# Attention with a decay bias and two MLP layers: no bias tile, the mask written into the broadcast sum, query tiles from last to first

## The chip, the cores and the metric

One core of a Trainium2 chip runs the whole program. The metric is the device time of one execution in microseconds; the median of several runs counts. TensorE (PE) does the matrix products and transposes, VectorE (DVE), ScalarE (ACT) and GpSimd (POOL) the elementwise work, and SyncE (SP) issues all DMAs.

## The reference, cut to what matters

```python
# q, k, v: (4, 8, 576, 64), s: (4, 8, 576), float32
scores = 1/sqrt(64) * q @ k^T
cum  = cumsum(maximum(s, 0))                  # along the sequence
bias = -(cum[..., :, None] - cum[..., None, :])
scores = where(causal, -1e9, scores + minimum(bias, 0.0))
attn = exp(scores - max(scores)); attn /= sum(attn) + 1e-9
x = (attn @ v)  ->  (2304, 512)
y = (sigmoid(x @ w_gate) * (x @ w_val)) @ w_out        # d_ff 1536
h = y @ w_in                                            # d_ff 2048
out = (h - tanh(h)) @ w_out2
```

`cum` never falls along the sequence, so for every key that the causal mask leaves, the bias is at most zero and the minimum changes nothing. And a term that is the same for all keys of one query drops out of the softmax.

## The kernel before

The weights are 64-bit words; a `Conversion` turns each into a pair of fp32r parts (high and low), one unit of 128x512 per tick: two passes on ScalarE (L96, L82), three on VectorE (L88, L89, L91) and one on GpSimd (L83). The first conversion has 24 units (`w_gate`, `w_val`); its ticks are spread over the first 32 attention steps (`CONV_AT`).

Attention runs in 64 units (batch, query group, head). Group 0 holds queries 0 to 255 as two tiles, t = 0 and 1, against 256 keys; group 1 holds queries 256 to 575 as three tiles, t = 2, 3, 4, against 576 keys. All units of group 0 come first, batch by batch, then those of group 1. A tile is a step; there are 160. A tile t sees `width(t)` = 128, 256, 384, 512 or 576 keys, and only its last 128 columns need the causal mask. The loop over steps is written out by hand, and each engine gets its instructions in that order. In iteration i the program issues:

- VectorE: `eps(i-1)`, the score pass `ttr(i)` (L236: product in PSUM plus bias tile, scaled by -0.125, with the running minimum), `recip(i-1)`, `norm(i-1)`, the evacuation `evac(i-2)` of the transposed probabilities into a low part (L287, after ScalarE's high part L286), `nb(i+2)`, then `gt` of a gate product (L363), `xp` of a finished unit (L316), and the conversion's passes.
- GpSimd: `norm(i-1)` for t = 3 and 4 (L259; VectorE does it for the others, L261), the causal select of `nb(i+2)` (L206), the splits of x, v, k and q (L325, L186, L168, L172), and the conversion's low part (L83).
- ScalarE: high part of `evac(i-2)`, `exp(i)` (L243), `xtmp` (L315), high parts of the splits, the conversion's passes.
- TensorE: `qk(i+1)` (L223, L224), one or two gate or value products (`moe`, L347 to L351) of the batch finished last, the transposes `tr(i-1)` (L273), and the value product `pv` (L300) of a unit whose last evacuation has been issued. After the first 16 steps the transposes of all steps share one bank (bank 6), so `tr(i-1)` waits for `evac(i-2)` as well as for `norm(i-1)`.

The bias tile is made by `nb(i)` in two instructions: VectorE computes min(c - cum_i, 0) from `c`, the broadcast cumulative sum (loaded once per unit, three buffers), and `cumn`, a column of negated sums; GpSimd then fills the masked triangle of the last 128 columns. The sums are scaled by 8 (L379) to undo the factor of 0.125 on the way. `cumn` is made once, by five transposes of `cum` on TensorE (L384) and a copy on VectorE (L390). The transposed probabilities of a unit lie in one pair of buffers (`NPT = 1`) of five slots; group 0 uses slots 0 and 3, and relies on zeros in the part of slot 3 that no query of the first tile sees.

After attention come the rest of the products of the last batch, the output projection with conversion of `w_out` and `w_in` (to about 600 us), and the second layer.

Of the kernel before, what the change touches and what calls it, by code (L numbers as in the profile page):

```python
# [21 lines left out]
GRP = ((0, 256, (0, 1)), (256, 320, (2, 3, 4)))  # L22
MASK = -8.0e9
LN = 1
NSP = 3
# [13 lines left out]
def NORM(G, t):  # L39
    return "pool" if t > 2 else "dve"  # L40
# [3 lines left out]
def attention_moe_moe2(ctx: ExitStack, tc: tile.TileContext, kqT, v, s, wg, wv, wo, win, wo2, out):  # L44
# [11 lines left out]
    class Conversion:  # L56
        """float64 words to an exact pair of float32r parts of the float32 value, one unit per tick in three stages"""
# [138 lines left out]
    def nb(i):  # L196
        if i >= len(steps):
            return
        u, t = steps[i]
        b, G, h = units[u]  # L200
        w = width(t)
        n = at.tile([128, S], F, tag="nb", name="nb", bufs=3)[:, :w]
        c = U_[u]["c"][:, 0:w]
        j = b * H + h
        DVE.tensor_scalar(out=n, in0=c, scalar1=cumn[:, t, j:j + 1], scalar2=0.0, op0=ALU.add, op1=ALU.min)  # L205
        POOL.affine_select(out=n[:, w - 128:w], in_=n[:, w - 128:w], pattern=[[-1, 128]], base=0,  # L206
                           channel_multiplier=1, compare_op=ALU.is_ge, fill=MASK)
        T_[i] = {"nb": n}

    def qk(i):  # L210
# [8 lines left out]
        T_[i]["qk"] = []  # L219
# [7 lines left out]
    def ttr(i):  # L227
# [6 lines left out]
        for k, (ps, c0, c1) in enumerate(e.pop("qk")):  # L234
            init, acc = acc, e["nm"][:, k:k + 1]
            DVE.tensor_tensor_reduce(out=sp[:, c0:c1], in0=ps[:, 0:c1 - c0], in1=e["nb"][:, c0:c1],  # L236
# [39 lines left out]
    def evac(i):  # L276
# [8 lines left out]
        js = slice(0, t + 1) if G else slice(0, 3 * t + 1, 3)  # L285
# [5 lines left out]
    def pv(u):  # L291
# [5 lines left out]
        jobs = [(0, 0, 0), (1, 3, 0)] if G == 0 else [(0, 0, 0), (1, 1, 0), (2, 2, 0), (3, 3, 64), (4, 4, 64)]  # L297
# [77 lines left out]
    cumn = pt.tile([128, 5, 32], F, name="cumn")  # L375
    DVE.memset(zt, 0.0)
    DVE.tensor_scalar(out=sraw, in0=sraw, scalar1=0.0, scalar2=None, op0=ALU.max)
    DVE.tensor_tensor_scan(out=cum, data0=sraw, data1=zt, initial=0.0, op0=ALU.add, op1=ALU.add)
    DVE.tensor_scalar(out=cum, in0=cum, scalar1=8.0, scalar2=None, op0=ALU.mult)  # L379
    SP.dma_start(out=cscr, in_=cum)  # L380
    load_vc(0)
    ps = bank(6, [128, 5, 32])
    for t in range(5):
        PE.transpose(ps[:, t, :], cum[:, Q0[t]:Q0[t] + 128], ident[0:32, 0:32])  # L384
# [5 lines left out]
    DVE.tensor_scalar(out=cumn, in0=ps, scalar1=-1.0, scalar2=None, op0=ALU.mult)  # L390
    for _ in range(PRE):
        cvt.tick()
    nb(0)
    nb(1)
    split_v(0)
    split_kq(1)
    while parts:
# [7 lines left out]
    for i in range(n + LN + 1):  # L405
# [15 lines left out]
        if i < n:  # L421
            exp(i)
            nb(i + 2)
# [248 lines left out]
```

## Time and profile before

| | us |
|---|---|
| median of 3 runs (1157.55 to 1158.14) | 1157.69 |
| span of the profiled execution | 1156.5 |
| TensorE busy in it | 1063.0 |
| VectorE busy | 724.9 |
| ScalarE busy | 539.2 |
| GpSimd busy | 391.1 |

The profiled execution is one execution apart from the timed ones; its span runs from the first to the last instruction, and a run's time holds a little around that. Shares of busy time over the whole span say little here, because the stages have different limits; the views below are therefore cut by stretches: 0 to 136 us holds the first 32 steps with the conversion, 136 to 236 us the rest of group 0, 236 to 545 us group 1.

### The profile page before, as it was taken

How to read it: one execution, taken by the hardware profiler on the slowest of the kernel's cores; microseconds unless marked ns; L12 is line 12 of the kernel's file. 1: busy time of each engine (PE TensorE's matmuls, PEld its weight loads, DVE VectorE, ACT ScalarE, POOL GpSimd, SP SyncE). 2: the span in 40 equal slices, each digit the busy share in tenths (PEclk: the TensorE clock that was granted, in tenths of full speed). 3: DMA queues.
4: the chain of work that ended last, by engine and by line, in shares of the span. 5: the costliest groups of instructions: out<-in, count | busy, mean ns of one | idle time of the engine just before them, and what ended most of it. 6: DMA issues, size and time to landing. Idle time of an engine off the chain costs nothing.

```text
span 1156.5 us, 18998 instructions
## 1 busy us (share of the span) xinstructions
PE 1063.0 (92%) x6501; PEld 997.0 (86%) x6501; DVE 724.9 (63%) x1783; ACT 539.2 (47%) x1325; POOL 391.1 (34%) x524
## 2 busy tenths in 40 slices
PE   3457799989999999999899999999999999999998
PEld 2346699989899899898889999997899999999997
DVE  7999967688878788873856677378423233232322
ACT  4565556566666666653434444344323232232322
POOL 6786645466656566651311222023000000000000
PEclk9999999999999999999999999999999999999999
DMA  6556444443433433321746655233000000000000
GB/s 190 163 161 176 115 119 127 135 144 114 132 120 124 120 125 120 119 77 40 231 146 180 185 167 172 71 96 106 28 1 28 1 22 6 1 28 1 28 1 28
DMA packets 64417, 114.11 MB, mean 99 GB/s; under 512 B 7168, under 2 KB 40960, under 8 KB 64320
## 3 DMA queue, kind: packets, MB, share of 16 engines
q1 hardware_dynamic: 64320, 112.90, 31.8%
q8 instruction: 51, 0.84, 0.3%
q14 instruction: 46, 0.38, 0.1%
HBM read 93.92 MB, written 18.95 MB: 98 GB/s over the span
## 4 chain that ended last, share of the span: by engine, by line
PE 72%; DVE 15%; issue 5%; DMA 3%; ACT 3%; SPq 0%; POOL 0%; DVEq 0%; ACTq 0%; POOLq 0%
PE bank L605 15%; PE bank L348 6%; PE bank L347 6%; PE bank L351 6%; PE bank L581 5%; PE bank L582 5%; PE bank L585 5%; PE bank L300 4%; DVE raw L89 4%; PE bank L548 4%; PE bank L549 4%; PE bank L552 4%; PE bank L273 4%; PE bank L223 2%; DMA raw<-in_wo 2%
## 5 line engine op out<-in xcount | busy, mean ns | idle before, releaser
L588 DVE TENSOR_TENSOR th<-bank,th 128x384 f32<-128x384 f32 x96 | 53.5, 557 | 196.2 <-ACT th L587 196.1
L273 PE MATMUL bank<-ident,sp 128*128 128x128 f32 (+1 forms) x480 | 78.6, 273 | 68.8 <-DVE ptl L287 35.2
L286 ACT ACTIVATE pth<-bank 128x320 fp32r<-128x320 f32 (+2 forms) x160 | 69.6, 435 | 146.8 <-PE bank L300 88.1
L587 ACT ACTIVATE th<-bank 128x384 f32<-128x384 f32 x96 | 46.9, 488 | 192.0 <-PE bank L585 192.0
L273 PEld LDWEIGHTS bank<-ident,sp 128*128 128x128 f32 (+1 forms) x480 | 51.8, 143 | 86.6 <-DVE ptl L287 37.7
L243 ACT ACTIVATE sp<-sp,nm 128x576 f32<-128x576 f32 (+2 forms) x160 | 95.9, 599 | 45.0 <-DVE nm L236 44.8
L287 DVE TENSOR_TENSOR ptl<-bank,pth 128x320 fp32r<-128x320 f32 (+2 forms) x160 | 77.6, 485 | 49.0 <-ACT pth L286 33.0
L206 POOL TENSOR_SCALAR_AFFINE_SELECT nb<-nb 128x128 f32<-128x128 f32 x160 | 48.0, 300 | 150.9 <-DVE nb L205 115.1
L592 DVE TENSOR_TENSOR g2l<-th,g2h 128x384 fp32r<-128x384 f32 x96 | 53.6, 558 | 56.7 <-ACT g2h L591 56.7
L591 ACT ACTIVATE g2h<-th 128x384 fp32r<-128x384 f32 x96 | 50.4, 525 | 62.4 <-DVE th L588 62.4
L205 DVE TENSOR_SCALAR nb<-cbc,cumn 128x576 f32<-128x576 f32 (+2 forms) x160 | 76.6, 479 | 2.2 <-DMA cbc<-cum 2.2
L236 DVE CUSTOM_DVE_ANT_0 sp<-bank,nb 128x288 f32<-128x288 f32 (+2 forms) x160 | 75.6, 472 | 1.2 <-POOL nb L206 0.2
L223 PE MATMUL bank<-kh,qs 128*128 128x384 f32 (+1 forms) x192 | 70.7, 373 | 6.0 <-POOL qs L172 6.0
L89 DVE SCALAR_TENSOR_TENSOR raw<-raw 128x512 uint32<-128x512 uint32 x68 | 74.2, 1091 | 2.3
L496 DVE TENSOR_TENSOR gl<-g,gh 128x384 fp32r<-128x384 f32 x72 | 39.6, 556 | 57.3 <-PE bank L552 38.1
L261 DVE TENSOR_SCALAR sp<-sp,r 128x128 f32<-128x128 f32 (+1 forms) x96 | 72.6, 756 | 3.4
L168 POOL TENSOR_TENSOR kl<-kq,kh 128x256 fp32r<-128x256 f32 (+1 forms) x64 | 73.0, 1141 | 3.6 <-ACT kh L167 2.8
L300 PE MATMUL bank<-pth,vs 128*128 128x256 f32 (+1 forms) x224 | 71.2, 335 | 0.6 <-ACT pth L286 0.6
L495 ACT ACTIVATE gh<-g 128x384 fp32r<-128x384 f32 x72 | 37.1, 526 | 71.2 <-PE bank L549 60.8
L96 ACT ACTIVATE tmp<-raw 128x512 f32<-128x512 f32 x68 | 45.5, 669 | 46.6 <-DMA raw<-in_wo 26.8
L300 PE MATMUL bank<-ptl,vs 128*128 128x256 f32 (+1 forms) x224 | 64.7, 309 | 0.1
L91 DVE SCALAR_TENSOR_TENSOR tmp<-tmp,raw 128x512 uint32<-128x512 uint32 x68 | 59.9, 881 | 6.0 <-DVE raw L89 0.5
(588 smaller groups left out, 3405.3 us busy)
## 6 DMA issues: line engine op xcount, KB each, us to landing
kq<-in_kq SPq DMA_DIRECT2D x32, 448.0 KB, 3.6
raw<-in_wo SPq DMA_DIRECT2D x28, 512.0 KB, 3.6
g<-g SPq DMA_DIRECT2D x72, 192.0 KB, 3.4
cbc<-cum SPq DMA_DIRECT2D x32, 288.0 KB, 4.0
kq<-in_kq SPq DMA_DIRECT2D x32, 256.0 KB, 3.5
raw<-in_win SPq DMA_DIRECT2D x16, 512.0 KB, 3.6
g<-gt SPq DMA_DIRECT2D x48, 160.0 KB, 1.8
raw<-in_wg SPq DMA_DIRECT2D x12, 512.0 KB, 4.4
```

What stands on the lines that cost most here:

```text
L89: DVE.scalar_tensor_tensor(out=lo, in0=lo, scalar=29, in1=hi, op0=ALU.logical_shift_right, op1=ALU.bitwise_or)
L168: POOL.tensor_tensor(out=kl, in0=d["k"], in1=kh.bitcast(F), op=ALU.subtract)
L205: DVE.tensor_scalar(out=n, in0=c, scalar1=cumn[:, t, j:j + 1], scalar2=0.0, op0=ALU.add, op1=ALU.min)
L223: PE.matmul(ps, d["qs"][:, o:o + 128], d["kh"][:, c0:c1], start=True, stop=False)
L236: DVE.tensor_tensor_reduce(out=sp[:, c0:c1], in0=ps[:, 0:c1 - c0], in1=e["nb"][:, c0:c1], scale=-0.125, scalar=init, op0=ALU.add, op1=ALU. ...
L243: ACT.activation(out=e["sp"], in_=e["sp"], func=AF.Exp, scale=-1.0, bias=e["m"], accum_out=e["sum"])
L261: DVE.tensor_scalar(out=e["sp"], in0=e["sp"], scalar1=e["r"], scalar2=None, op0=ALU.mult)
L273: PE.transpose(ps[:, j, :], e["sp"][p0:128, c:c + 128], ident[p0:128, p0:128])
L286: ACT.activation(out=ph[:, js, o:o + n], in_=e["tr"], func=AF.Copy)
L287: DVE.tensor_tensor(out=pl[:, js, o:o + n], in0=e["tr"], in1=ph[:, js, o:o + n].bitcast(F), op=ALU.subtract)
L300: PE.matmul(ps[:, o:qw], d["vs"][:, j].rearrange("p a d -> p (a d)"), p[:, slot, o:qw], start=(n == 0 and m == 0), stop=(n == len(jobs) - ...
L605: PE.matmul(acc[t], g[:, t * 128:t * 128 + 128], w, start=(m == 0 and k == 0), stop=(m == M2 - 1 and k == 2))
```

## The change

- `nb` is gone, with `cumn`, its transposes, and the bias buffers. The score pass reads `c` itself: the sum of the query drops out of the softmax, and the minimum with zero does nothing where the mask leaves a key.
- The mask is written into `c` in place, one select per step as before (`mask(i+1)` in iteration i, ahead of `exp(i)`). So that a masked triangle hides no key that a later tile of the head needs, the tiles of a head go from last to first: 1, 0 and 4, 3, 2.
- All norms are on VectorE (`NORM`), those of t = 3 and 4 too.
- Group 0 uses slots 0 and 3 in even units and 1 and 4 in odd ones; a memset on GpSimd clears slot 4's part once at the start of group 1.
- The scaling by 8 moves into the maximum ahead of the cumulative sum, and MASK becomes a power of two. `sp` has five buffers instead of three.

```diff
-GRP = ((0, 256, (0, 1)), (256, 320, (2, 3, 4)))
-MASK = -8.0e9
+GRP = ((0, 256, (1, 0)), (256, 320, (4, 3, 2)))
+MASK = -(2.0 ** 33)
-NSP = 3
+NSP = 5
...
 def NORM(G, t):
-    return "pool" if t > 2 else "dve"
+    return "dve"
...
-    def nb(i):
-        if i >= len(steps):
-            return
-        u, t = steps[i]
-        b, G, h = units[u]
-        w = width(t)
-        n = at.tile([128, S], F, tag="nb", name="nb", bufs=3)[:, :w]
-        c = U_[u]["c"][:, 0:w]
-        j = b * H + h
-        DVE.tensor_scalar(out=n, in0=c, scalar1=cumn[:, t, j:j + 1], scalar2=0.0, op0=ALU.add, op1=ALU.min)
-        POOL.affine_select(out=n[:, w - 128:w], in_=n[:, w - 128:w], pattern=[[-1, 128]], base=0,
-                           channel_multiplier=1, compare_op=ALU.is_ge, fill=MASK)
-        T_[i] = {"nb": n}
+    def mask(i):
+        if i < len(steps):
+            u, t = steps[i]
+            w = width(t)
+            c = U_[u]["c"][:, w - 128:w]
+            POOL.affine_select(out=c, in_=c, pattern=[[-1, 128]], base=0, channel_multiplier=1,
+                               compare_op=ALU.is_ge, fill=MASK)
...
-            DVE.tensor_tensor_reduce(out=sp[:, c0:c1], in0=ps[:, 0:c1 - c0], in1=e["nb"][:, c0:c1],
+            DVE.tensor_tensor_reduce(out=sp[:, c0:c1], in0=ps[:, 0:c1 - c0], in1=U_[u]["c"][:, c0:c1],
...
-        js = slice(0, t + 1) if G else slice(0, 3 * t + 1, 3)
+        js = slice(0, t + 1) if G else slice(u % 2, u % 2 + 3 * t + 1, 3)
...
-    cumn = pt.tile([128, 5, 32], F, name="cumn")
     DVE.memset(zt, 0.0)
-    DVE.tensor_scalar(out=sraw, in0=sraw, scalar1=0.0, scalar2=None, op0=ALU.max)
+    DVE.tensor_scalar(out=sraw, in0=sraw, scalar1=0.0, scalar2=8.0, op0=ALU.max, op1=ALU.mult)
     DVE.tensor_tensor_scan(out=cum, data0=sraw, data1=zt, initial=0.0, op0=ALU.add, op1=ALU.add)
-    DVE.tensor_scalar(out=cum, in0=cum, scalar1=8.0, scalar2=None, op0=ALU.mult)
...
-    ps = bank(6, [128, 5, 32])
-    for t in range(5):
-        PE.transpose(ps[:, t, :], cum[:, Q0[t]:Q0[t] + 128], ident[0:32, 0:32])
...
-    DVE.tensor_scalar(out=cumn, in0=ps, scalar1=-1.0, scalar2=None, op0=ALU.mult)
...
-    nb(0)
-    nb(1)
+    mask(0)
...
+        if i - LN - 1 >= 0 and i - LN - 1 < n and steps[i - LN - 1] == (B * H, 4):
+            for p in pts[0]:
+                POOL.memset(p[:, 4, 128:256].bitcast(F), 0.0)
...
         if i < n:
+            mask(i + 1)
             exp(i)
-            nb(i + 2)
```

In the rows of the order below, the names after `<-` are what an instruction reads; `ISA` is the score pass and, in the row after it, the read of its minimum. First VectorE in the first batch, from the score pass of a unit's second tile to that of the next unit's first; before:

```order
L236 ISA sp,nm<-bank_399,nb 128x256
L236 ISA nm 128x1
L252 RECIPROCAL r<-sum 128x1
L261 TENSOR_SCALAR sp<-sp,r 128x128
L287 TENSOR_TENSOR ptl_156<-bank_402,pth_155 128x2x128
L205 TENSOR_SCALAR nb<-cbc,cumn 128x256
L88 TENSOR_SCALAR raw<-raw 128x512
L89 SCALAR_TENSOR_TENSOR raw<-raw 128x512
L91 SCALAR_TENSOR_TENSOR tmp<-tmp,raw 128x512
L247 TENSOR_SCALAR sum<-sum 128x1
L236 ISA sp,nm<-bank_421,nb 128x128
```

and after the change:

```order
L230 ISA sp,nm<-bank_374,cbc 128x128
L230 ISA nm 128x1
L246 RECIPROCAL r<-sum 128x1
L255 TENSOR_SCALAR sp<-sp,r 128x256
L281 TENSOR_TENSOR ptl_156<-bank_377,pth_155 128x128
L88 TENSOR_SCALAR raw<-raw 128x512
L89 SCALAR_TENSOR_TENSOR raw<-raw 128x512
L91 SCALAR_TENSOR_TENSOR tmp<-tmp,raw 128x512
L241 TENSOR_SCALAR sum<-sum 128x1
L230 ISA sp,nm<-bank_393,cbc 128x256
```

The nb row between the evacuation and the conversion is gone, the score pass reads `cbc` (the tile `c`), and the narrow tile comes second in the unit instead of the wide one.

Next GpSimd, one unit of the first batch, with the engines that each instruction waits for in brackets (`Activation` is ScalarE, `DMAHW` a load); before:

```order
L206 AFFINE_SELECT nb_684<-nb_684 128x128 [waits DVE_49]
L186 TENSOR_TENSOR vs_619<-vraw_546,vs_619 128x2x64 [waits DMAHW6_49,PE_49,Activation_49]
L168 TENSOR_TENSOR kl_696<-kq_620,kh_695 128x256 [waits DMAHW0_49,Activation_49]
L172 TENSOR_TENSOR qs_697<-kq_620,qs_697 64x256 [waits Activation_49,Pool_49]
L206 AFFINE_SELECT nb_726<-nb_726 128x128 [waits DVE_49,Pool_49]
L83 TENSOR_TENSOR w03l_95<-tmp_593,w03h_94 128x512 [waits Activation_49]
```

and after:

```order
L201 AFFINE_SELECT cbc_514<-cbc_514 128x128 [waits DVE_49]
L186 TENSOR_TENSOR vs_582<-vraw_513,vs_582 128x2x64 [waits DMAHW6_49,PE_49,Activation_49]
L168 TENSOR_TENSOR kl_655<-kq_583,kh_654 128x256 [waits DMAHW0_49,Activation_49]
L172 TENSOR_TENSOR qs_656<-kq_583,qs_656 64x256 [waits Activation_49,Pool_49]
L201 AFFINE_SELECT cbc_586<-cbc_586 128x128 [waits DMAHW1_49,Pool_49]
L83 TENSOR_TENSOR w03l_95<-tmp_558,w03h_94 128x512 [waits Activation_49]
```

The selects stand at the same places, but the first now waits for the score pass that reads the same `c`, and the second, which belongs to the next unit, waits for the load of its `c` and no longer for VectorE.

Last VectorE in group 1, two steps; before:

```order
L287 TENSOR_TENSOR ptl_156<-bank_6133,pth_155 128x4x128
L205 TENSOR_SCALAR nb<-cbc,cumn 128x576
L247 TENSOR_SCALAR sum<-sum 128x1
L236 ISA sp,nm<-bank_6171,nb 128x512
L236 ISA nm 128x1
L252 RECIPROCAL r<-sum 128x1
L261 TENSOR_SCALAR sp<-sp,r 128x384
L287 TENSOR_TENSOR ptl_156<-bank_6187,pth_155 128x5x64
L205 TENSOR_SCALAR nb<-cbc,cumn 128x384
L363 SCALAR_TENSOR_TENSOR gt<-th,bank_6174 128x320
```

and after:

```order
L230 ISA sp,nm<-bank_6085,cbc 128x512
L230 ISA nm 128x1
L246 RECIPROCAL r<-sum 128x1
L255 TENSOR_SCALAR sp<-sp,r 128x576
L281 TENSOR_TENSOR ptl_156<-bank_6088,pth_155 128x3x128
L241 TENSOR_SCALAR sum<-sum 128x1
L230 ISA sp,nm<-bank_6109,cbc 128x384
L246 RECIPROCAL r<-sum 128x1
L255 TENSOR_SCALAR sp<-sp,r 128x512
L281 TENSOR_TENSOR ptl_156<-bank_6125,pth_155 128x5x64
```

An nb behind each evacuation is gone, and a norm stands ahead of each, those of 576 and 512 columns being new on this engine; before, only the norm of 384 columns stood there.

## Rows read from the trace of the kernel before

**Rows 1.** The head of the profile's page.

```profile
span 1156.5 us, 18998 instructions
```

**Rows 2.** Busy time of each engine in stretches of the span: start and end in us, length, then busy us (and instructions) of PE, PEld, DVE, ACT and POOL, granted TensorE clock, DMA share, GB/s.

```profile
8.00:136.00 128.00, 67.48 (x418) 60.04 (x417) 119.36 (x315) 73.92 (x221) 91.23 (x112) 1.00 0.55 165
136.00:148.00 12.00, 10.83 (x78) 10.63 (x79) 10.80 (x43) 8.52 (x31) 7.96 (x15) 0.86 0.43 111
148.00:236.00 88.00, 85.46 (x714) 84.76 (x712) 60.88 (x239) 50.53 (x175) 43.77 (x80) 1.00 0.46 130
236.00:300.00 64.00, 59.44 (x458) 56.19 (x459) 55.78 (x168) 42.48 (x106) 41.59 (x60) 1.00 0.40 125
300.00:545.00 245.00, 238.29 (x1662) 226.99 (x1661) 188.56 (x579) 147.41 (x366) 140.26 (x204) 0.99 0.35 107
600.00:1156.50 556.50, 550.76 (x2859) 508.94 (x2857) 244.69 (x386) 192.60 (x384) 44.36 (x32) 1.00 0.20 63
```

**Rows 3.** The waits of PE, the first two rows in 8 to 136 us, the third in 300 to 545 us: who waited for whom, us in total, times, longest.

```profile
PE bank L273 <- DVE sp L261: 30.8, 16, 2.9
PE bank L273 <- DVE ptl L287: 20.5, 12, 4.1
...
PE bank L273 <- DVE ptl L287: 5.5, 6, 1.6
```

**Rows 4.** The chain of waits in the first batch, one stretch of two units (42 to 54.8 us), the nb instructions on it: start us, us on the chain, what.

```profile
46.76 0.54 DVE nb L205
...
50.93 0.26 DVE nb L205
...
53.07 0.54 DVE nb L205
```

**Rows 5.** The same view in the second batch, one stretch of two units (102.6 to 122.5 us), the nb instructions on it.

```profile
105.71 0.96 DVE nb L205
...
110.77 0.19 DVE nb L205
...
116.30 0.26 DVE nb L205
...
121.07 0.19 DVE nb L205
```

**Rows 6.** Groups of instructions by form in 8 to 136 us, of VectorE and, in the last two rows, ScalarE: line, engine, operation, names, shapes, count, busy us, mean ns of one, idle before.

```profile
L205 DVE TENSOR_SCALAR nb<-cbc,cumn 128x256 f32<-128x256 f32 x16 | 10.3, 645 | 0.0
L236 DVE CUSTOM_DVE_ANT_0 sp<-bank,nb 128x256 f32<-128x256 f32 x16 | 6.6, 415 | 0.2
L205 DVE TENSOR_SCALAR nb<-cbc,cumn 128x128 f32<-128x128 f32 x17 | 5.6, 327 | 2.2 <-DMA cbc<-cum 2.2
L236 DVE CUSTOM_DVE_ANT_0 sp<-bank,nb 128x128 f32<-128x128 f32 x16 | 4.5, 278 | 0.2 <-POOL nb L206 0.2
...
L243 ACT ACTIVATE sp<-sp,nm 128x256 f32<-128x256 f32 x16 | 8.1, 505 | 12.5 <-DVE nm L236 12.5
L243 ACT ACTIVATE sp<-sp,nm 128x128 f32<-128x128 f32 x16 | 6.4, 400 | 28.6 <-DVE nm L236 28.6
```

**Rows 7.** The timeline from 28 to 33 us, some instructions of VectorE and GpSimd: start us, us, engine, line, operation.

```profile
28.48 0.69 DVE L89 SCALAR_TENSOR_TENSOR raw<-raw 128x512 uint32<-128x512 uint32 x1
28.57 1.72 POOL L83 TENSOR_TENSOR w01l<-tmp,w01h 128x512 fp32r<-128x512 f32 x1
29.21 1.63 DVE L91 SCALAR_TENSOR_TENSOR tmp<-tmp,raw 128x512 uint32<-128x512 uint32 x1
31.22 0.35 DVE L261 TENSOR_SCALAR sp<-sp,r 128x256 f32<-128x256 f32 x1
32.04 0.29 POOL L206 TENSOR_SCALAR_AFFINE_SELECT nb<-nb 128x128 f32<-128x128 f32 x1 [1.75 <-DVE nb L205]
```

**Rows 8.** The chain of waits at the start.

```profile
5.76 0.81 DVE cumsum L379
...
11.10 5.23 DMA kq<-in_kq
```

**Rows 9.** VectorE in 300 to 545 us: first the norm of 384 columns (shortest, median and longest in ns), then groups by form.

```profile
L261 DVE TENSOR_SCALAR sp<-sp,r x24: 421/1291/1657, 306.5 to 526.1; 128x384 f32<-128x384 f32 x24
...
L205 DVE TENSOR_SCALAR nb<-cbc,cumn 128x576 f32<-128x576 f32 x24 | 12.2, 510 | 0.0
L205 DVE TENSOR_SCALAR nb<-cbc,cumn 128x384 f32<-128x384 f32 x24 | 12.0, 499 | 0.0
L205 DVE TENSOR_SCALAR nb<-cbc,cumn 128x512 f32<-128x512 f32 x24 | 11.9, 494 | 0.0
```

**Rows 10.** Two rows on the select: the longest wait of the whole span that GpSimd has (us in total, times, longest), and the page's group of the score pass, whose last number is how long it waited for the select.

```profile
POOL nb L206 <- DVE nb L205: 115.1, 124, 4.8
...
L236 DVE CUSTOM_DVE_ANT_0 sp<-bank,nb 128x288 f32<-128x288 f32 (+2 forms) x160 | 75.6, 472 | 1.2 <-POOL nb L206 0.2
```

**Rows 11.** The timeline in group 1, from 402 and from 410 us, some instructions of three engines.

```profile
402.81 1.43 POOL L168 TENSOR_TENSOR kl<-kq,kh 128x576 fp32r<-128x576 f32 x1
...
403.17 1.29 DVE L261 TENSOR_SCALAR sp<-sp,r 128x384 f32<-128x384 f32 x1
...
410.66 0.69 DVE L287 TENSOR_TENSOR ptl<-bank,pth 128x512 fp32r<-128x512 f32 x1 [0.42 <-ACT pth L286]
...
412.09 0.52 PE L273 MATMUL bank<-ident,sp 64*128 64x64 f32 x5
```

More of the change, by code (lines that the diff above doesn't have):

```diff
@@ L218, in qk @@
         cuts = [(0, max(w, 256))] if t < 4 else [(0, 288), (288, 576)]
-        T_[i]["qk"] = []
+        T_[i] = {"qk": []}
         for c0, c1 in cuts:
@@ L296, in pv @@
         ps = bank(7, [128, qw])
-        jobs = [(0, 0, 0), (1, 3, 0)] if G == 0 else [(0, 0, 0), (1, 1, 0), (2, 2, 0), (3, 3, 64), (4, 4, 64)]
+        jobs = [(0, u % 2, 0), (1, 3 + u % 2, 0)] if G == 0 else [(0, 0, 0), (1, 1, 0), (2, 2, 0), (3, 3, 64), (4, 4, 64)]
         for n, (j, slot, o) in enumerate(jobs):
@@ L454, in attention_moe_moe2 @@
             xq.append((steps[e][0], pv(steps[e][0])))
-        if i < n and t == 4 and vparts:
+        if i < n and t == 2 and vparts:
             vparts.pop(0)()
@@ L458, in attention_moe_moe2 @@
             moe(*mq.pop(0))
-        if CONV_AT(i):
+        for _ in range(CONV_AT(i)):
             cvt.tick()
```

## The prediction

> **What bounds the kernel now.** I read the stretches first. [rows 2] cut the span where the work changes. From 8 to 136 us TensorE is busy 67.48 of 128 us and VectorE 119.36: this is the stretch in which the first two batches of the first query group run beside the conversion of the gate and value weights. In every later attention stretch TensorE is nearly full: 85.46 of 88, 59.44 of 64, 238.29 of 245. After 600 us comes code that the diff does not touch (550.76 of 556.5). So VectorE sets the pace up to 136 us, TensorE from there on, and a VectorE instruction removed has two very different prices. The waits of TensorE say the same: 30.8 and 20.5 us before 136 us, for the norm (L261) and the evacuation (L287), against 5.5 us for the evacuation in the long stretch of the second group [rows 3]. Then I read the chain of waits: in the first batch two units have three nb instructions on it, 0.54, 0.26 and 0.54 us [rows 4]; in the second batch two units have four, 0.96, 0.19, 0.26 and 0.19 us [rows 5]. Last, the lines by form give the price of each operation [rows 6, 9].
>
> **The change, part by part.** Times are set against the profiled execution, whose span is 1156.5 us [rows 1]; the median of the runs is 1157.69 us, 1.2 us more for what lies around the span. A difference of spans is carried over to the median.
>
> *The nb instruction up to 136 us.* 16 instructions of 0.645 us and 17 of 0.327 us go, 15.9 us of VectorE's busy time [rows 6]. On the chain they are worth less. First batch: 8 units are 4 pairs, each 0.54 + 0.26 + 0.54 = 1.34 us, 5.4 us in all. Second batch: 4 pairs of 0.96 + 0.19 + 0.26 + 0.19 = 1.60 us, 6.4 us. Sum 11.8 us. Two things are given back.
> (a) With the wide tile first, the iteration that ends in the xp instruction runs the longer way round: score pass (L236) 0.415 instead of 0.278 us, exp 0.505 instead of 0.400 us, and only then xtmp on ScalarE, for which xp waits [rows 6]. That is 0.24 us more per unit where ScalarE decides, as it does in the first batch: 8 x 0.24 = 1.9 us. VectorE's own work in a unit is the same, only in another order.
> (b) Part of an nb is not work but standing still. [rows 7] show it: the conversion's L91 on VectorE, begun at 29.21 while GpSimd's L83 runs from 28.57 to 30.29, lasts 1.63 us, where the similar L89 before it, of the same shape, lasts 0.69 us; and a scaling of 128x256, the nb's shape, lasts 0.35 us at 31.22, where GpSimd stands still until 32.04. So of the 0.96 us instruction some 0.6 us is waiting for GpSimd, and half of that may pass on to the conversion two instructions later: 4 x 0.3 = 1.2 us.
> 11.8 - 1.9 - 1.2 = 8.7 us. Bounds: if all blocked time passes on, only free prices are saved, 0.35 us for each of 16 wide instructions, or 5.6 us, less (a): 3.7 us; if all of the busy time is saved, 15.9 us. I take 8.7, because the chain is the nearest row to what ends last.
>
> The Trainium skill's page "SBUF — State Buffer", section "Who interferes with whom", states that VectorE instructions in a two-port mode, and those with two SBUF inputs, share a pair of ports with GpSimd under a lock that is held for the whole instruction. The rows at 29 us agree. By that rule the score pass, which has one input in PSUM, is not touched, the nb instruction is, and so is every norm that the change brings to VectorE: the rule counts 160 contenders gone and 64 new ones, and the latter are the third rival below; without the lock the new norms would cost their free price everywhere, and the sum would be mine.
>
> *Start.* The second scaling of cum (L379, 0.81 us) stands on the chain ahead of the store of cum, and goes; the transposes into cumn and the copy stand beside the loads. The chain runs on through a load of kq that takes 5.23 us [rows 8]. I take 0.8 us; the ends are 0 (the load is held by the other transfers) and 0.8.
>
> *The mask in place.* A select of the same shape stays (160 of them on GpSimd), now one step ahead instead of two. Within a unit it waits for the score pass of the step before, since it writes the tile which that pass reads; behind it on GpSimd are the splits of v, k and q and the conversion's low part. Now the same queue stands still for nb instead, 115.1 us in 124 waits, while the score pass as good as never waits for the select (0.2 us) [rows 10]. The new release (end of the score pass) comes earlier in VectorE's order than the old one (nb, behind norm and evacuation), so GpSimd is held less, not more. The score pass that reads the mask is a whole step later. At nothing, therefore; if GpSimd were late by one select of 0.3 us [rows 7] in each step up to 136 us, it would cost 32 x 0.3 = 9.6 us. The two memsets at the change of groups hold GpSimd for one matmul group, once: under 1 us, hidden because the next mask is for the next unit.
>
> *Second group.* From 300 to 545 us, 72 nb of 0.510, 0.494 and 0.499 us go: 36.1 us [rows 9]. In their place VectorE gets some 49 norms of 512 and 576 columns that GpSimd did. Their price is not in the trace: free, by nb of the same widths, 0.5 us (24.5 us in all); blocked, by the median of the norm of 384 columns that VectorE does already, 1.291 us (63.3 us). VectorE's load moves by -11.6 to +27.2 us, of 188.56 busy in 245: it still fits. Inside an iteration the norm stands ahead of the evacuation for which TensorE's next transpose waits. [rows 11] give the slack: the evacuation that starts at 410.66 ends at 411.35, the transposes start at 412.09, so 0.74 us is free, and a norm of 0.5 us put ahead fits, beside the 0.5 us that nb gives back. The long split of k (kl, 1.43 us) met the norm of tile 2 at 402.81 and 403.17; it will now meet that of tile 4, one such meeting per unit as before, behind a score pass of the same 512 columns. I take 0 for the new norms.
>
> *What TensorE can still win after 136 us.* It idles 12 - 10.83, 88 - 85.46, 64 - 59.44 and 245 - 238.29 us, 15.0 us together [rows 2]. How much of it nb had a hand in, the rows do not tell apart. The slots that alternate in the first group free its evacuation from the value product before, in a stretch where TensorE idles 2.5 us at most. I take a tenth, 1.5 us; ends: 15 us of gain, and the loss of the third rival.
>
> Sum: 8.7 + 0.8 + 1.5 = 11.0 us, 1157.7 - 11.0 = **1146.7 us**.
>
> **Rivals.**
> *First: all of nb comes back, and more.* GpSimd, no longer tied to nb, works ahead, and blocked time falls too. 15.9 + 0.8 + 4 us (a good quarter of the idle of TensorE) = 20.7 us, **1137 us**. For it: the 115.1 us that GpSimd waits. Against: it is busy 91.23 of 128 us in the first stretch [rows 2], and wherever it runs it meets the conversions.
> *Second: the blocked time only moves on.* 3.7 + 0.8 + 0 = 4.5 us, **1153 us**. For it: 0.6 us of a 0.96 us nb is not work. Against: most nb on the chain are 0.19 to 0.54 us, near the free price.
> *Third, on the other side: the norms of the second group are late.* If two norms per unit, not one, meet a split on GpSimd and last 1.65 us, the longest of the present ones [rows 9], instead of 0.5, and nb gives nothing back on the path, the transpose is late by 1.15 - 0.74 = 0.4 us each, on TensorE's path: 32 units x 2 x 0.4 = 25.6 us, less 9.5 of gain: +16 us, **1174 us**. With one more per unit it is 12.8 - 9.5 = +3.3 us, 1161 us; it decides from a delay of 0.74 us upward. For it: the only norm that VectorE does there lasts 1.291 us in the median, three times the 0.421 us of its shortest. Against: kl has only one norm to meet per unit, as before, and GpSimd loses its own norms.
> *Fourth: the select is late* (9.6 us from above): 11.0 - 9.6 = 1.4 us of gain, **1156.3 us**, no change. Against it: the wait of 0.2 us.
>
> **How the numbers follow.** My case 0.55, first rival 0.15, second 0.12, third 0.11, fourth 0.07. No difference of less than 0.2%, 2.3 us, can be told from no change here. Faster: 0.55 + 0.15 + 0.12 = 0.82. Same: 0.07, and 0.02 of the third, where little is late: 0.09. Slower: 0.09. The range runs from the first rival to the fourth, 1137 to 1156.5 us, and leaves out the third and some of the first's tail.
>
> **What would show it.** Right: the stretch up to the last conversion is shorter by 8 to 10 us, with VectorE still the fullest engine there; the attention after it is as long as before to 2 us; the score pass waits for the select under 3 us in all; the norms of 512 and 576 columns last under 0.9 us in the mean. Second rival: L89 and L91 grow as nb goes. Third: TensorE waits for norm or evacuation over 12 us after 236 us. Fourth: the score pass waits for the select by some 10 us. The forecast is wrong if the shortening lies elsewhere than before 136 us.

## The result and the profile after

| | before | after |
|---|---|---|
| median, us (4 runs each, side by side) | 1157.91 (1157.55 to 1158.53) | 1169.88 (1169.09 to 1170.93) |
| span of the profiled execution | 1156.5 | 1167.3 |

The ratio is 1.0104, interval 1.009 to 1.0118: the kernel became slower by 12.0 us, where 11 us of gain were forecast. The head of the page after, and then the stretches of [rows 2], with the same columns:

```profile
span 1167.3 us, 18790 instructions
```

```profile
8.00:136.00 128.00, 69.45 (x427) 61.58 (x427) 114.14 (x286) 75.33 (x225) 93.24 (x114) 1.00 0.53 166
...
148.00:236.00 88.00, 84.62 (x707) 83.74 (x706) 54.81 (x211) 49.20 (x171) 43.58 (x79) 1.00 0.43 126
236.00:300.00 64.00, 56.94 (x434) 53.34 (x434) 49.62 (x149) 39.89 (x100) 30.81 (x45) 1.00 0.39 121
300.00:545.00 245.00, 233.14 (x1617) 220.52 (x1618) 186.60 (x554) 148.24 (x367) 113.44 (x156) 0.99 0.34 106
```

Up to 136 us VectorE is still nearly full (114.14 of 128). In the second group TensorE, which should be the bound, is busy 5.15 us less in the same 245 us.

Such windows cut at fixed times; to see where time goes, the same event must be compared. A unit ends with its value product (L300 before, L294 after), so the start of that product in the timeline marks each unit. The last column is the mended kernel of the experiments (run f2).

| start of the value product, us | before | after | mended |
|---|---|---|---|
| first unit | 21.30 | 22.08 | 21.99 |
| fifteenth | 136.38 | 134.71 | 134.69 |
| first of the second group | 245.57 | 244.24 | 240.09 |
| last | 535.15 | 548.36 | 532.86 |
| end of the span | 1156.5 | 1167.3 | 1150.4 |

After against before, stretch by stretch: +0.8 at the start, -2.5 from the first unit to the fifteenth, +0.3 in the rest of the first group, +14.5 in the second group (289.6 to 304.1), -2.4 behind attention; before rounding the sum is +10.8, the difference of the spans. In the third batch of the second group units took 9.58 and 9.39 us by turns before, and 10.21 and 9.50 after.

The waits of TensorE up to 136 us, and from 300 to 545 us, as in [rows 3]:

```profile
PE bank L267 <- DVE sp L255: 30.4, 17, 3.4
PE bank L267 <- DVE ptl L281: 22.4, 14, 4.2
```

```profile
PE bank L267 <- DVE ptl L281: 6.5, 5, 2.0
PE bank L267 <- DVE sum L241: 5.4, 9, 0.9
```

The first two are as long as before: taking nb away shortened none of them. The fourth is new. It names `eps` (L241), the next instruction on VectorE, but what the transposes wait for stands just before it. The norms of the second group on VectorE, 300 to 545 us by form, answer to [rows 9]:

```profile
L255 DVE TENSOR_SCALAR sp<-sp,r 128x576 f32<-128x576 f32 x25 | 36.0, 1440 | 0.9
L255 DVE TENSOR_SCALAR sp<-sp,r 128x512 f32<-128x512 f32 x25 | 12.7, 507 | 0.9
L255 DVE TENSOR_SCALAR sp<-sp,r 128x384 f32<-128x384 f32 x24 | 11.3, 469 | 0.9
```

Two of three norms are at their free price; the one of 576 columns, the first tile of the unit, takes 1440 ns. The timeline at one of them shows how the norm meets the split of k:

```profile
372.10 1.78 DVE L255 TENSOR_SCALAR sp<-sp,r 128x576 f32<-128x576 f32 x1
372.12 1.44 POOL L168 TENSOR_TENSOR kl<-kq,kh 128x576 fp32r<-128x576 f32 x1 [1.68 <-ACT kh L167]
...
373.79 0.54 DVE L281 TENSOR_TENSOR ptl<-bank,pth 128x384 fp32r<-128x384 f32 x1
...
374.39 0.52 PE L267 MATMUL bank<-ident,sp 64*128 64x64 f32 x5
```

The split of k on GpSimd and the norm begin together; the norm ends 0.32 us after the split, and the evacuation and the five transposes stand behind it. This is one of the short units (9.51 us): TensorE's products end at 374.35, so it loses next to nothing. The same place in one of the long units (10.21 us, its value product starts at 404.80):

```profile
402.06 1.45 POOL L168 TENSOR_TENSOR kl<-kq,kh 128x576 fp32r<-128x576 f32 x1
402.24 1.59 DVE L255 TENSOR_SCALAR sp<-sp,r 128x576 f32<-128x576 f32 x1
...
403.02 0.75 PE L345 MATMUL bank<-xl,w00h 128*128 128x320 f32 x4
...
403.75 0.54 DVE L281 TENSOR_TENSOR ptl<-bank,pth 128x384 fp32r<-128x384 f32 x1
...
404.35 0.52 PE L267 MATMUL bank<-ident,sp 64*128 64x64 f32 x5 [0.57 <-DVE sum L241]
```

Here the products end at 403.77, the evacuation behind the norm ends at 404.29, and TensorE stands still for 0.57 us.

Two explanations were open. **K**: the split of k holds the norm of 576 columns, and that costs the time. **O**: the descending order itself makes the way through a unit longer. A third, **N**, was that norms of 512 and 576 columns don't belong on VectorE at all.

### The profile page after: what moved, and what is told of

It is laid out like the page before. It is cut to its first block, busy times and chain, and to the rows that moved or that the text cites. A ratio compares the mean times of both kernels' runs of the same rounds, so it can differ in the third digit from the quotient of the medians.

```text
span 1167.3 us, 18790 instructions
## 1 busy us (share of the span) xinstructions
PE 1066.5 (91%) x6496; PEld 998.1 (86%) x6496; DVE 708.3 (61%) x1685; ACT 540.9 (46%) x1325; POOL 356.4 (31%) x462
## 4 chain that ended last, share of the span: by engine, by line
PE 67%; DVE 17%; issue 6%; ACT 4%; DMA 4%; SPq 0%; POOL 0%; DVEq 0%; ACTq 0%; POOLq 0%
PE bank L595 15%; PE bank L571 5%; PE bank L572 5%; PE bank L575 5%; PE bank L341 5%; PE bank L342 5%; PE bank L345 5%; PE bank L294 5%; PE bank L538 4%; PE bank L542 4%; PE bank L539 4%; DVE raw L89 3%; PE bank L267 3%; DVE sp L230 3%; DVE sp L255 3%
## 5 line engine op out<-in xcount | busy, mean ns | idle before, releaser
L267 PE MATMUL bank<-ident,sp 64*128 64x64 f32 (+1 forms) x480 | 79.3, 274 | 77.6 <-DVE ptl L281 38.9
L280 ACT ACTIVATE pth<-bank 128x384 fp32r<-128x384 f32 (+2 forms) x160 | 69.6, 435 | 157.0 <-PE bank L294 83.2
L267 PEld LDWEIGHTS bank<-ident,sp 64*128 64x128 f32 (+1 forms) x480 | 51.9, 143 | 98.0 <-DVE ptl L281 49.8
L237 ACT ACTIVATE sp<-sp,nm 128x384 f32<-128x384 f32 (+2 forms) x160 | 96.0, 600 | 48.3 <-DVE nm L230 48.0
L255 DVE TENSOR_SCALAR sp<-sp,r 128x384 f32<-128x384 f32 (+2 forms) x160 | 112.9, 706 | 5.7
L281 DVE TENSOR_TENSOR ptl<-bank,pth 128x384 fp32r<-128x384 f32 (+2 forms) x160 | 77.2, 483 | 54.8 <-ACT pth L280 54.6
L186 POOL TENSOR_TENSOR vs<-vraw,vs 128x128 fp32r<-128x128 f32 (+1 forms) x64 | 44.3, 693 | 143.3 <-ACT vs L185 143.2
L217 PE MATMUL bank<-kh,qs 128*128 128x288 f32 (+1 forms) x192 | 70.6, 373 | 13.0 <-POOL qs L172 13.0
L230 DVE CUSTOM_DVE_ANT_0 sp<-bank,cbc 128x384 f32<-128x384 f32 (+2 forms) x160 | 75.8, 473 | 9.8 <-POOL cbc L201 8.8
L89 DVE SCALAR_TENSOR_TENSOR raw<-raw 128x512 uint32<-128x512 uint32 x68 | 72.8, 1070 | 2.3
L201 POOL TENSOR_SCALAR_AFFINE_SELECT cbc<-cbc 128x128 f32<-128x128 f32 x160 | 59.0, 369 | 49.7 <-DVE r L246 41.6
L294 PE MATMUL bank<-pth,vs 128*128 128x256 f32 (+1 forms) x224 | 71.5, 337 | 0.7 <-ACT pth L280 0.7
L91 DVE SCALAR_TENSOR_TENSOR tmp<-tmp,raw 128x512 uint32<-128x512 uint32 x68 | 63.4, 933 | 4.8
L294 PE MATMUL bank<-ptl,vs 128*128 128x256 f32 (+1 forms) x224 | 64.3, 308 | 0.0
```

Of the source, the lines that this page charges most:

```text
L89: DVE.scalar_tensor_tensor(out=lo, in0=lo, scalar=29, in1=hi, op0=ALU.logical_shift_right, op1=ALU.bitwise_or)
L91: DVE.scalar_tensor_tensor(out=tmp, in0=tmp, scalar=3, in1=lo, op0=ALU.logical_shift_left, op1=ALU.bitwise_or)
L217: PE.matmul(ps, d["qs"][:, o:o + 128], d["kh"][:, c0:c1], start=True, stop=False)
L237: ACT.activation(out=e["sp"], in_=e["sp"], func=AF.Exp, scale=-1.0, bias=e["m"], accum_out=e["sum"])
L255: DVE.tensor_scalar(out=e["sp"], in0=e["sp"], scalar1=e["r"], scalar2=None, op0=ALU.mult)
L267: PE.transpose(ps[:, j, :], e["sp"][p0:128, c:c + 128], ident[p0:128, p0:128])
```

## The experiments

Each run stands beside runs of the kernel before on the same chip; their medians were 1158.51 us for the first four, 1158.05 for the next four and 1158.31 for the last four.

**e1: the norms back on GpSimd.**

```diff
 def NORM(G, t):
-    return "dve"
+    return "pool" if t > 2 else "dve"
```

> The changed kernel with the norms of tiles 3 and 4 back on GpSimd; all else as changed. Three theories for the loss of some 14 us in group 1. N (the norms on VectorE make its part of the loop too long): about 1156 us, the units of group 1 back at 9.4 us. K (the long split of k, kl, holds up the norm of the first tile of a unit, and that delay lies on the path to TensorE's transposes): no recovery, 1167 to 1175, since on GpSimd the norm of tile 4 stands in the queue right behind kl. O (the order of tiles: the wide score pass now follows the passage through ScalarE): no recovery, 1165 to 1172.

1170.95 us (2 runs), 1.0118 of before (1.0068 to 1.0167). Units of 10.15 and 9.46 us, as slow as after. TensorE now waits for the norm on GpSimd, where it stands behind the split of k in the queue (300 to 545 us):

```profile
PE bank L267 <- POOL sp L253: 6.2, 12, 0.8
```

N falls: on either engine the norm of the first tile is late by the same split.

**e2: the second group's tiles from first to last again.** **e3: that and the norms back on GpSimd**, as in e1.

```diff
-GRP = ((0, 256, (1, 0)), (256, 320, (4, 3, 2)))
+GRP = ((0, 256, (1, 0)), (256, 320, (2, 3, 4)))
...
-        if i < n and t == 2 and vparts:
+        if i < n and t == 4 and vparts:
```

> The changed kernel with the tiles of group 1 from first to last again. Part of the computation changes: the mask of tile 2 stays in the sum that tiles 3 and 4 read, so these lose keys. N: no recovery, 1168 to 1172 us. K: kl meets the norm of tile 2 (384 columns) as in the kernel before, so most comes back, 1155 to 1159. O: the same, 1155 to 1159.

> Both: tiles of group 1 from first to last and their norms of tiles 3 and 4 on GpSimd, so that in group 1 only the removal of nb is left of the change. Part of the computation changes as in the run above. N, K and O alike: 1154 to 1157 us, the loss gone and the 1.3 us that the time up to the first unit of group 1 gained kept. If it stays above 1162, the loss comes from the mask or from nb itself and all three fall.

e2: 1152.38 us (5 runs), 0.9955 (0.9936 to 0.9973). e3: 1151.62 us (4 runs), 0.9939 (0.991 to 0.9968). The whole loss is gone, and the time is 6 to 7 us below before. All units of the third batch but its last take 9.38 to 9.40 us. Yet the split still meets a norm, that of the unit's first tile, now 384 columns (e2, 300 to 545 us):

```profile
L255 DVE TENSOR_SCALAR sp<-sp,r 128x384 f32<-128x384 f32 x24 | 32.1, 1340 | 0.9
```

So 1.3 us there do not show in the units, and 1.4 us on the first tile of the descending order do, in every other unit. A meeting alone does not cost; it costs where TensorE runs out of work before the instructions behind the meeting are done.

**e4: the order of the splits turned round in the second group**, so that k's comes an iteration later.

```diff
-        parts.extend([part_k, part_q])
+        parts.extend([part_k, part_q] if q0 == 0 else [part_q, part_k])
```

> The changed kernel, but in group 1 the split of q is issued in the first iteration of a unit and that of k in the second, one step later than now. K: kl no longer meets the norm of 576 columns but that of 512, which stands in front of a longer stretch of TensorE work (the value product): most of the loss comes back, 1154 to 1160 us, and the norm of 576 columns falls from 1.67 us to under 0.9 us in the mean. O: no recovery, 1167 to 1171. N: no recovery.

1159.78 us (8 runs), 1.0012 (0.9998 to 1.0026): 10 of the 12 us are back. The meeting has moved on rather than gone:

```profile
L255 DVE TENSOR_SCALAR sp<-sp,r 128x512 f32<-128x512 f32 x24 | 27.8, 1157 | 0.8
L255 DVE TENSOR_SCALAR sp<-sp,r 128x576 f32<-128x576 f32 x24 | 23.2, 968 | 0.9
```

Units take 9.78 and 9.42 us. K is supported, but O is not yet excluded, since both norms are still held.

**f1: descending, without the split of k.**

```diff
-            POOL.tensor_tensor(out=kl, in0=d["k"], in1=kh.bitcast(F), op=ALU.subtract)
+            if q0 == 0:
+                POOL.tensor_tensor(out=kl, in0=d["k"], in1=kh.bitcast(F), op=ALU.subtract)
...
-            PE.matmul(ps, d["qs"][:, o:o + 128], d["kl"][:, c0:c1], start=False, stop=True)
+            PE.matmul(ps, d["qs"][:, o:o + 128], d["kl" if q0 == 0 else "kh"][:, c0:c1], start=False, stop=True)
```

> The kernel after the change, descending order, but in the second group the low part of k is not computed: GpSimd's split of k (24 times 1.43 us) is left out and the second product of each score tile reads the high part again, so TensorE's work is the same and the output differs. Theory K (the split of k on GpSimd holds up the norm of 576 columns, and that alone costs the time): norm of 576 columns back at about 0.55 us in the mean (1.67 in after), units of the second group at 9.40 us each, about 1152 us. Theory O (descending order itself makes the path through a unit longer than TensorE's work): the norm is short, but the units stay above 9.6 us in the mean, 1158 us or more. Between them: about 9.5 us per unit.

1152.38 us (3 runs), 0.9954 (0.9938 to 0.997). Norm of 576 columns 568 ns in the mean; units 9.58 and 9.39 us, as before the change, which is 9.5 in the mean, the value that the expectation put between the theories. The second group takes 292.7 us: leaving out the split gives back 11.4 of the 14.5 us. K holds, in the descending order. But O is not nothing: in the ascending order without nb (e2, e3) the second group takes 286.5 and 286.7 us, 6 us less than here (4 to 5 less, if it is counted from the last value product of the first group). The total hides this, because f1 reaches the first value product of the second group at 241.2 us and e2 at 244.8.

**f2: the same meeting avoided, nothing left out (the mended kernel).** The split is issued one iteration later, behind the select, which waits for the score pass; VectorE's norm follows that pass too, and is under way before the split comes to its turn.

```diff
         def part_k():
+            def low():
+                POOL.tensor_tensor(out=kl, in0=d["k"], in1=kh.bitcast(F), op=ALU.subtract)
             ACT.activation(out=kh, in_=d["k"], func=AF.Copy)
-            POOL.tensor_tensor(out=kl, in0=d["k"], in1=kh.bitcast(F), op=ALU.subtract)
+            if q0 == 0:
+                low()
+            else:
+                late.append(low)
...
             mask(i + 1)
+            while late:
+                late.pop(0)()
             exp(i)
```

> The kernel after the change with one instruction moved, nothing left out: in the second group GpSimd's split of k is issued one iteration later, directly behind the select, which waits for the score pass; VectorE's next norm then starts together with the select, ahead of the split. Theory K: the norm of 576 columns is short (under 0.8 us in the mean), units at 9.4 us, 1152 to 1154 us. Theory O: units stay above 9.6 us, 1158 us or more. If the split now meets the next norm (512 columns) instead, that norm shows 1 us or more in the mean and the result lies at about 1157 us.

1151.95 us (4 runs, 1151.25 to 1152.67), 0.9945 (0.993 to 0.996). The timeline at the place:

```profile
361.05 0.29 POOL L206 TENSOR_SCALAR_AFFINE_SELECT cbc<-cbc 128x128 f32<-128x128 f32 x1 [1.61 <-DVE r L251]
361.10 0.56 DVE L260 TENSOR_SCALAR sp<-sp,r 128x576 f32<-128x576 f32 x1
361.31 1.64 POOL L168 TENSOR_TENSOR kl<-kq,kh 128x576 fp32r<-128x576 f32 x1
361.86 0.56 DVE L286 TENSOR_TENSOR ptl<-bank,pth 128x384 fp32r<-128x384 f32 x1 [0.20 <-ACT pth L285]
```

The two instructions still overlap, but the norm is 0.21 us ahead: it takes 0.56 us instead of 1.78, and the split pays 0.20 us, which nobody waits for. Which of two instructions on two engines comes first is worth 1.2 us of VectorE here. In a long unit TensorE's transposes now follow its products without a gap (391.83). Units take 9.58 and 9.40 us, where K had 9.4, and the second group takes 292.8 us, still 3.2 more than before: what the mended kernel gains, it gains ahead of the second group (first value product at 240.09 us, before at 245.57).

**f3: the split of q put behind a select too**, that of the next unit's first iteration.

`lateq` takes up the split of q as `late` does that of k; on top of f2:

```diff
...
+            while first and lateq:
+                lateq.pop(0)()
...
```

> As the run before, and the split of q too is issued behind a select (that of the first iteration of the next unit), so that no two splits stand in a row on GpSimd in the second group. Nothing left out. Theory K: all three norms of the second group under 0.8 us in the mean, 1151 to 1153 us, at most 1 us better than the run before. Theory O: no better than 1158 us.

1155.8 us (8 runs, 1153.34 to 1157.11), 0.9976 (0.9965 to 0.9987): the expected 1151 to 1153 us were missed. The norms are as expected (606, 489 and 467 ns), the units are those of f2 to 0.02 us, and the second group takes 292.67 us against 292.77. The profiled execution lost its 3.6 us against f2 before that: 141.6 against 138.8 us at the sixteenth value product, 243.65 against 240.09 at the first of the second group, where TensorE's granted clock was lower (0.64 from 128 to 136 us and 0.72 from 136 to 144, against 0.79 and 1.00 in f2, shown below). Whether the edit has a part in that is open.

**f4: the kernel before, with the second group from last to first.**

```diff
-GRP = ((0, 256, (0, 1)), (256, 320, (2, 3, 4)))
+GRP = ((0, 256, (0, 1)), (256, 320, (4, 3, 2)))
...
-        if i < n and t == 4 and vparts:
+        if i < n and t == 2 and vparts:
```

> The kernel before, with its bias tiles, and only the order of the tiles of the second group turned round (4, 3, 2, with the split of v moved to the last tile of a unit as in the changed kernel). Nothing left out. If the order with the meeting of split and norm is what costs the time, this alone is slower than before: here the norms of 576 and 512 columns are on GpSimd, behind the split of k in its queue, and nb is still there, so 10 us or more slower, 1168 us or later. If the loss needs the removal of nb, it stays within 3 us of before.

1186.34 us (4 runs), 1.0241 (1.0224 to 1.0257), 28 us slower than before. The split at 359.45 lasts to 360.89; the norm behind it in GpSimd's queue starts at 360.87 and lasts 0.95 us; the transposes then come. TensorE's wait from 300 to 545 us:

```profile
PE bank L273 <- POOL sp L259: 16.3, 21, 1.5
```

The turn of the order is what costs, with or without nb. With nb it costs 28 us; without it, and with the norms on GpSimd too, 19 us (e1 against e3).

**g1: the mended kernel without the low parts of k and q in the first group.** It asks where the time of nb went up to 136 us. On top of f2:

```diff
-            if q0 == 0:
-                low()
-            else:
+            if q0:
                 late.append(low)
...
-            POOL.tensor_tensor(out=qs[64:128], in0=d["q"][64:128], in1=qs[64:128].bitcast(F), op=ALU.subtract)
+            if q0:
+                POOL.tensor_tensor(out=qs[64:128], in0=d["q"][64:128], in1=qs[64:128].bitcast(F), op=ALU.subtract)
...
-            PE.matmul(ps, d["qs"][:, o:o + 128], d["kl"][:, c0:c1], start=False, stop=True)
+            PE.matmul(ps, d["qs"][:, o:o + 128], d["kl" if q0 else "kh"][:, c0:c1], start=False, stop=True)
```

> The mended kernel (split of k behind the select in the second group) with the low parts of k and q left out in the first group: GpSimd's 32 splits of each are not issued there and the second product reads the high part again, so the output differs; TensorE's and ScalarE's work is the same. It asks where the bias tiles' time went up to 136 us. If it went into the conversion, which now meets those splits (L88 grew from 471 to 696 ns in the mean): L88 falls below 0.5 us, L89 and L91 fall by 0.1 to 0.3 us, and the way from the first to the fifteenth value product (112.7 us now, 115.1 before the change) becomes shorter by 8 us or more. If what limits there is the longer passage over ScalarE or the order of the tiles, it becomes shorter by less than 3 us.

From the first to the fifteenth value product 111.1 us, 1.6 less than f2 (112.7): the 8 us did not come. The conversion's three passes, 21 to 134 us by form, in before, after and g1:

```profile
L91 DVE SCALAR_TENSOR_TENSOR tmp<-tmp,raw 128x512 uint32<-128x512 uint32 x22 | 25.3, 1151 | 1.5
L89 DVE SCALAR_TENSOR_TENSOR raw<-raw 128x512 uint32<-128x512 uint32 x22 | 21.6, 983 | 0.8
L88 DVE TENSOR_SCALAR raw<-raw 128x512 uint32<-128x512 uint32 x22 | 10.4, 471 | 0.1
```

```profile
L91 DVE SCALAR_TENSOR_TENSOR tmp<-tmp,raw 128x512 uint32<-128x512 uint32 x22 | 28.4, 1290 | 0.8
L89 DVE SCALAR_TENSOR_TENSOR raw<-raw 128x512 uint32<-128x512 uint32 x22 | 19.8, 902 | 0.8
L88 DVE TENSOR_SCALAR raw<-raw 128x512 uint32<-128x512 uint32 x22 | 15.3, 696 | 0.1
```

```profile
L91 DVE SCALAR_TENSOR_TENSOR tmp<-tmp,raw 128x512 uint32<-128x512 uint32 x22 | 31.5, 1433 | 0.8
L89 DVE SCALAR_TENSOR_TENSOR raw<-raw 128x512 uint32<-128x512 uint32 x22 | 22.6, 1029 | 0.8
L88 DVE TENSOR_SCALAR raw<-raw 128x512 uint32<-128x512 uint32 x21 | 10.0, 478 | 0.1
```

The three together: 57.3, 63.5 and 64.1 us, the last with one L88 fewer in the window. L88 did fall to 478 ns in g1, so it is those splits that held it; but what it gave up, L89 and L91 took, now against the conversion's own L83. Half of the expectation held, the half that matters for the time did not. By the expectation's own bound, less than 3 us speaks for the longer way or the order of the tiles as what limits there; as the three passes together did not become shorter, the run does not show what the stretch would take without their waiting. The whole run took 1146.39 us (2 runs), 0.9908 (0.9887 to 0.9929); against f2 its first unit came 1.7 us earlier, the fifteenth 3.3, and the rest lies behind that.

**g2: the mended kernel with the first group in ascending order.** On top of f2:

```diff
-GRP = ((0, 256, (1, 0)), ...
+GRP = ((0, 256, (0, 1)), ...
```

> The mended kernel with the tiles of the first group in ascending order again (0, 1), so that the mask of the first tile hides keys from the second and the output differs. It prices the term of the prediction for the wide tile first (1.9 us up to 136 us). If the term is right, the way from the first to the fifteenth value product becomes shorter by 1 to 3 us (from 112.7 to about 110.5). If the order does not matter there, it stays within 0.5 us.

From the first to the fifteenth value product 110.3 us, 2.4 less than f2. The term of the prediction for the wide tile first (1.9 us) holds in size. Part of it is again a meeting: L88 took 605 ns in the mean, not 698. The whole run took 1150.28 us (2 runs), 0.9942 (0.9921 to 0.9963).

**g3: the selects ahead of the splits; f2 once more beside it.**

In the second unit the splits of k and q both go to `late`; on top of f2:

```diff
...
-            mask(i + 1)
+            if not (G == 0 and t == 0 and steps[i + 1][0] < B * H):
+                mask(i + 1)
+            if first and G == 0 and steps[i + 2][0] < B * H:
+                mask(i + 2)
             while late:
                 late.pop(0)()
```

> The mended kernel, nothing left out, with the selects freed from the queue of splits: the splits of the second unit are issued behind the select of the second step, and in the first group the select of the next unit's first tile is issued a step earlier, ahead of the splits. If the score pass of the first steps is late because the select stands behind the splits on GpSimd (1.24 and 0.92 us of wait), the first value product comes 1 to 2 us earlier (at about 20.5 us instead of 22.0) and the time falls by 1 to 2 us, to about 1150.5. If other things hold the start, nothing changes.

> The mended kernel once more, with more rounds, as the measure beside the run with the freed selects: 1151 to 1153 us, faster than before by 0.4 to 0.7 per cent.

g3: 1154.62 us (11 runs), 0.9973 (0.996 to 0.9985). f2 again: 1153.37 us (9 runs), 0.9967 (0.9954 to 0.9979). The first unit ends at 21.26 us, 0.7 earlier than in f2, so the select behind the splits did hold the start. But the way to the fifteenth became 115.8 us, 3.1 more: L89 went from 901 to 1308 ns in the mean, L91 from 1290 to 1002, and the three passes together from 63.6 to 66.4 us between these two value products. The new queue on GpSimd put other meetings into each unit, and they cost more than the start gave. f2, 0.55 and 0.33 per cent faster than before in its two runs (the second a little above its expectation), has the lowest times of the complete kernels, though its second interval and that of g3 overlap.

## Why the prediction was wrong, by its own steps

**The second group: wrong, and this is the failure.** The step was: "it will now meet that of tile 4, one such meeting per unit as before, behind a score pass of the same 512 columns. I take 0 for the new norms." The count was right. The price was carried over from a place where the meeting is hidden to one where it is not: the unit's first tile had been that of 384 columns, and e2 shows 1340 ns there at no cost that its units show (9.39 us); with the tile of 576 columns first, 1440 ns cost 11.4 of the 14.5 us lost in the group: f1 leaves out the split alone and f2 moves it alone, and both take these back. The other 3.1 us are the order without the meeting: it takes some 6 us more than the ascending order (292.7 against 286.5 us), and in the ascending order the removal of nb had given 3 (289.6 to 286.5). The slack of 0.74 us of [rows 11] was read for the transposes of tile 4 in the ascending order, behind the evacuation of 512 columns; in the new order they stand behind another evacuation and behind the norm. The reversal of this group was priced nowhere in the sum. Why the ascending order hides the same delay was not tested; from the order alone, tile 4's two score products on TensorE follow the meeting there, and the narrow tile's here.

**The third rival** had the mechanism (a norm that meets a split and comes late) and the size (1161 to 1174 us), but got 0.11, because I made it need one meeting more than before. The one that there was sufficed. That its size fits is partly luck: it set 25.6 us of loss against 9.5 of gain, and the runs show 14.5 of loss in the second group and 2.5 of gain up to the fifteenth value product.

**The rule that spoke against the change.** A norm beside a split takes 1.78 or 0.56 us according to which of the two comes first, and the other of the pair waits. The Trainium skill, page "SBUF — State Buffer", section "Who interferes with whom", says this of a VectorE instruction in a two-port mode beside one on GpSimd: the one that issues first has the port pair for the whole instruction. The trace agrees, as far as the lengths tell which came first (see the last section). The score pass, for which the page expects no contention, takes 0.54 us for 384 columns at 374.72 beside a split of q that runs from 374.11 to 374.98 (after), while the conversion's L91 takes 1.64 us at 50.62 beside L83 from 50.17 to 51.72 (g1). I weighed that rule and gave its outcome the small chance.

**nb up to 136 us: right sign, too large.** Forecast 8.7 us, found 2.5, below the lower end of 3.7. Of 13.3 us of nb between 21 and 134 us, the conversion took 6.2 back (57.3 to 63.5). Term (b), 1.2 us, was the mis-sized one: it is 5.0 of the 6.2 us that are missing, term (a) is 0.5. Between the first and the fifteenth value product VectorE is busy 4.59 us less than before (105.88 against 110.47) and idle 2.14 us more (6.75 against 4.61). The exchange can be read in a single unit, before and then after:

```profile
46.42 0.73 POOL L172 TENSOR_TENSOR qs<-kq,qs 64x256 fp32r<-64x256 f32 x1
46.68 0.62 DVE L205 TENSOR_SCALAR nb<-cbc,cumn 128x256 f32<-128x256 f32 x1
47.22 0.43 DVE L88 TENSOR_SCALAR raw<-raw 128x512 uint32<-128x512 uint32 x1
```

```profile
46.73 0.73 POOL L172 TENSOR_TENSOR qs<-kq,qs 64x256 fp32r<-64x256 f32 x1
46.92 0.83 DVE L88 TENSOR_SCALAR raw<-raw 128x512 uint32<-128x512 uint32 x1
```

nb had sat out the split of q; without it L88 sits it out. Term (a), 1.9 us, was right (2.4 in g2). The second rival, "the blocked time only moves on", fits what the rows show in this stretch; that the stretch would be shorter without the passes' waiting was not shown (g1).

**Start: wrong sign.** Forecast -0.8, found +0.8. The store of cum moved from 6.60 to 6.26 us only, since the scan ahead of it, now beside two splits instead of one, took 1.84 instead of 1.35 us. Then the score pass waited for the select, in three waits up to 136 us:

```profile
DVE sp L230 <- POOL cbc L201: 5.4, 3, 3.3
```

The longest is that of the first score pass at 11.67, and not the select's doing: GpSimd itself waited 4.21 us for the load of `c`. The other two, 1.24 us at 14.98 and 0.92 us at 18.93, are selects that stand behind the splits. That is the fourth rival's mechanism, twice, in the first two units, and g3 took 0.7 us of it back; from there to 136 us the step "at nothing" was right.

**What TensorE can still win: right in sign, seen only when mended.** From the 31st value product to the first of the second group f2 takes 12.5 us, before 15.5.

## What to carry to other kernels

An instruction that waits for another engine most of its time is worth less than its busy time: ask which instruction will stand in its place beside the same neighbour. When the order of work is turned round, price every meeting of two engines anew at its new place, with what stands behind it; the number of meetings alone does not give the price. Where a meeting costs, look for a wait that both engines share already (here the score pass) and issue the long instruction behind it.

## What the runs showed of the hardware

At 372.10 the norm's record opens 0.02 us before that of the split, and yet the norm is the one that waits; with 0.21 us of lead (f2) it is not. Two records that open within some hundredths of a microsecond do not tell which instruction goes first; their lengths do.

Two profiled executions of the mended kernel differ by 3.2 us of span (1150.4 and 1153.6), with the same units in the steady stretches. Of this 1.5 us arise where TensorE passes from waiting for VectorE to full load, and 2.0 behind the last value product. Stretches from 128 to 144 us, f2 and then f2 again:

```profile
128.00:136.00 8.00, 4.79 (x28) 4.50 (x29) 7.20 (x21) 5.21 (x17) 6.20 (x8) 0.79 0.10 28
136.00:144.00 8.00, 6.67 (x58) 6.47 (x57) 6.32 (x26) 5.79 (x21) 5.58 (x12) 1.00 0.55 135
```

```profile
128.00:136.00 8.00, 3.55 (x25) 3.35 (x26) 7.20 (x21) 5.26 (x17) 6.25 (x8) 0.95 0.09 28
136.00:144.00 8.00, 7.03 (x49) 6.82 (x48) 5.61 (x24) 5.22 (x20) 4.38 (x10) 0.83 0.54 122
```

The granted clock (0.79 and 0.83 are mixtures of the levels of 1.2 and 2.4 GHz) was low in the first while TensorE had little to do, and in the second when it was needed: from the fifteenth value product to the sixteenth it took 4.13 us in the one, 5.66 in the other. A comparison of single profiles by a microsecond or two is therefore made between events on the same side of this place.

Behind attention the kernels without nb took 617 to 620 us against 621.35 before. That is not the work of nb: f4, which keeps it, took 618.4, and the two executions of the mended kernel differ by 2.0 us there (617.5 and 619.6). The difference lies ahead of the output projection, whose first product starts 60.8 us after the last value product in the kernel before, and 58.4 and 60.3 in the two executions of the mended one; the granted clock from that value product to 600 us was 0.95, 0.97 and 0.95. So the 2.4 us that the table shows behind attention count for nothing in the account of the change.
